# Pooled attention feeding a GELU feed-forward layer: w_in loaded in halves, and w_out with four rows in a run

## The chip, the cores and the metric

The kernel runs on one core of one Trainium2 chip. The metric is device microseconds from launch to end, lower is better; three runs of the kernel before gave 311.11, 311.66 and 311.69 us, median 311.66. Engine names are those of the profile: PE (matrix multiplications), PEld (the loading of their weights), DVE, ACT, POOL, and SP, which here only issues transfers.

## The reference, cut to what matters

Eight batches, eight heads, sequence 576, head size 64. Keys and values are pooled by means of 8 rows (576 to 72), attention is computed against the pooled rows, and the result, 4608 tokens by 512 channels, goes through two matrices with a GELU between them.

```python
k_p = k.reshape(B, H, Sp, pool, D).mean(axis=3)      # pool = 8, Sp = 72
v_p = v.reshape(B, H, Sp, pool, D).mean(axis=3)
scores = scale * np.matmul(q, k_p.transpose(0, 1, 3, 2))
attn = softmax(scores)                               # written out in the reference
x = np.matmul(attn, v_p)                             # then (B * S, H * D) = 4608 x 512
h = x @ w_in                                         # 512 x 2048
g = 0.5 * h * (1.0 + np.tanh(c * (h + 0.044715 * h * h * h)))
out = g @ w_out                                      # 2048 x 512, float32
```

## The kernel before, in words

**Stages.** The tokens are handled in nine groups of 512 (NG). Phase 1 of a group (`p1_mm`, L280 to L283) multiplies w_in by x: for each of 16 blocks of 128 hidden channels (fo) it accumulates four matmuls (ko, 128 input channels each). The weights of such a matmul are 128 columns of `w_in_b[:, ko, ...]`, the moving operand is 512 tokens of `xT`. `gelu` (L285) takes each block from PSUM to `gT`. Phase 2 (`p2_mm`, L290) multiplies `gT` by `w_out_b`: for each of four row blocks r it accumulates 16 matmuls, one for each fo, and `store` (L294) copies and writes the rows. The attention of batch nb = g + 1 is woven into group g: pooling additions on DVE (`k_steps`, `v_steps`, L145), transposes (`trans_k` L172, `trans_q` L189), scores (`qk` L211), exponentials (`expo` L218), weighted sums (`av` L231, for batch 0 L236), and the division (`norm`, `mult`).

**The start.** Batch 0 comes first. Sixteen dummy matmuls (`spin`, L312) open PE's program, and some more stand between the first transposes and scores. Then a loop over eight pairs (c, pr) runs `av`, `norm` and `mult` of batch 0; after pair 5 it issues 4, after pair 6 six and after pair 7 six of the sixteen "early" phase 1 matmuls of group 0 (L335 and L346: fo 0 to 3, first all with ko 0, then ko 1, and so on, 288 of the 512 tokens). Group 0 then does the other 224 tokens of fo 0 to 3, and fo 4 to 15 in full, with the pooling of batch 1 (DVE) and its transposes at set places in between. After pair 3 SP is given the loads of v for batch 1 (L345).

**The order of the work.** Each engine runs its instructions in the order in which the kernel writes them (`manual_schedule`, L46); waits are put in by the tile framework, which records which part of a tile an instruction reads or writes and makes a reader wait for the transfers that write a part it overlaps. Transfers that POOL issues share one software queue, and each uses the next of eight semaphores in turn, so that the ninth waits until the first has landed.

**Transfers that POOL issues at the start, in order (before):** q of batch 0 in two halves (L84), w_in columns 0 to 511 and 512 to 1023 (L103), then after five memsets k of batch 1 (L70, L71), q of batch 1, w_in columns 1024 to 1535 and 1536 to 2047, and w_out in four pieces of 512 rows (L139), then q of batch 2. SP issues half of k and all of v of batch 0, and v of batch 1. Both matrices are float32 in memory and bfloat16 in the tiles; the transfer converts them. One row of a w_in piece is 512 float32 values in memory, and so is a row of w_out: each run of a transfer reads 2 KB and writes 1 KB.

**Which piece which block needs (before).** w_in piece i serves fo 4i to 4i + 3. w_out piece i serves fo 4i to 4i + 3, and the first 32 matmuls of phase 2 in group 0 go through the pieces in that order (L419).

Of the kernel before, what the change touches and what calls it, by code (L numbers as in the profile page):

```python
# [18 lines left out]
def kernel(  # L19
# [9 lines left out]
    nc = tc.nc  # L29
# [29 lines left out]
    PS = psp.tile([128, 8, 512], F32, name="PS")  # L59
# [21 lines left out]
    def load_q(b, i0=0, i1=2):  # L81
        if b not in qs:
            qs[b] = qp.tile([128, 2, T * D], BF16, name="qb")
        nc.gpsimd.dma_start(  # L84
            out=qs[b][:, i0:i1],
            in_=q[b].rearrange("(i h) (p t) d -> (h p) i (t d)", i=2, t=T)[:, i0:i1])

    w_in_b = consts.tile([128, KO, DF], BF16, name="w_in_b")
    w_out_b = consts.tile([128, FO, DM], BF16, name="w_out_b")
    w_in_v = moe_w_in.rearrange("(ko p) f -> p ko f", p=128)  # L90
    w_out_v = moe_w_out.rearrange("(fo p) d -> p fo d", p=128)
    identb = consts.tile([128, 128], BF16, name="identb")


# [5 lines left out]
    make_identity(nc, identb)  # L100

    def load_w_in(i):
        nc.gpsimd.dma_start(out=w_in_b[:, :, i * 512:(i + 1) * 512], in_=w_in_v[:, :, i * 512:(i + 1) * 512])  # L103

    load_w_in(0)
    load_w_in(1)


    xT = consts.tile([128, KO, N], BF16, name="xT")
# [23 lines left out]

    load_k(1, [nc.gpsimd])
    load_q(1)
    load_w_in(2)
    load_w_in(3)
    for i in range(4):
        nc.gpsimd.dma_start(out=w_out_b[:, 4 * i:4 * i + 4, :], in_=w_out_v[:, 4 * i:4 * i + 4, :])  # L139


    qTs = {}
# [123 lines left out]
    def x_bank(g):  # L266
        return g % 2

    def h_bank(g, fo):
        x, y = x_bank(g), 1 - x_bank(g)  # L270
        if fo == 4:
            return 7
        return (x, 2, 3, y)[fo if fo < 4 else (fo - 1) % 4]
# [5 lines left out]

    def p1_mm(g, fo, ko, c0=0, c1=GROUP):  # L280
        r0 = g * GROUP
        nc.tensor.matmul(out=PS[:, h_bank(g, fo), c0:c1], lhsT=w_in_b[:, ko, fo * 128:(fo + 1) * 128],  # L282
                         rhs=xT[:, ko, r0 + c0:r0 + c1], start=(ko == 0), stop=(ko == KO - 1))  # L283

    def gelu(g, fo):  # L285
# [50 lines left out]
    for i, (c, pr) in enumerate(ORDER):  # L336
        bank = (4, 6, 0, 2, 4, 6, 4, 6)[i]
        av(0, c, pr, bank)
        norm(0, c, pr, bank)
        mult(0, c, pr, bank)  # L340
        if i == 3:

            vs[1] = kvp.tile([Sp, H, 512], F32, name="vt")
            nc.vector.memset(vs[1][:, 0, 0:1], 0.0)
            load_v(1, nc.sync)  # L345
        for fo, ko in early[:take[i]]:  # L346
            p1_mm(0, fo, ko, 0, CH)
        early = early[take[i]:]


    for g in range(NG):
# [34 lines left out]
        for fo, ko, c0 in first:  # L386
            p1_mm(g, fo, ko, c0)
        for fo in range(FO):
            if fo >= 4:
                for ko in range(KO):  # L390
                    p1_mm(g, fo, ko)
            gelu(g, fo)
            for s in side[fo]:
                s()
# [64 lines left out]
```

## Time and profile before

| what | value |
|---|---|
| time of the profiled execution | 311.66 us |
| its span, first to last instruction | 309.9 us |
| median of the three runs | 311.66 us |
| PE busy | 296.7 us, 96% |
| ACT busy, DVE busy | 220.9 us (71%), 157.1 us (51%) |
| phase 1 matmuls (L282), 128x512 | 379 ns each by the record, one every 216 ns |
| weight loads for them (L282, PEld) | 592 recorded, 98 ns each |
| transfers | 41.05 MB moved; 36.70 MB read, 9.44 MB written to memory |

The profiled execution's time is 1.8 us longer than its span. The matmuls overlap in PE's pipeline: a record of 379 ns includes the drain, and the starts of two matmuls of 512 tokens are 216 ns apart (seven of them make 1.51 us on the chain of waits). The weight loads run beside the matmuls. Landing times from the trace, in us from the start of the span (issue plus time to landing):

| transfer | issued | landed |
|---|---|---|
| w_in columns 0 to 511 | 3.0 | 16.6 |
| w_in columns 512 to 1023 | 3.8 | 18.6 |
| k of batch 1, main part | 8.1 | 21.7 |
| q of batch 1 | 9.2 | 25.8 |
| w_in columns 1024 to 1535 | 9.9 | 31.9 |
| w_in columns 1536 to 2047 | 10.7 | 36.6 |
| w_out, pieces 0, 1, 2, 3 | 11.8, 16.9, 18.9, 22.0 | 39.2, 41.6, 44.1, 46.7 |

### The profile page before, as it was taken

The page shows a single profiled execution, that of the slowest core. Times are in us where ns is not written, and L with a number is a line of the kernel's source. Part 1 is how long each engine was busy: PE and PEld are TensorE (multiplying, and loading weights), DVE is VectorE, ACT ScalarE, POOL GpSimd, SP SyncE. Part 2 cuts the span into 40 slices and gives each one's busy share as a digit, 9 for nine tenths or more (in the row PEclk, how much of TensorE's full clock was granted, in tenths as well). Part 3 has the DMA queues.
Part 4 walks back from the last instruction along what each step waited for, and adds up shares of the span by engine and source line. Part 5 has one row for each costly group of instructions (what it writes and reads, how often), then busy time and mean ns, then how long its engine had stood idle before and what let it go on. Part 6 is the DMA issues. An engine that isn't in the chain of part 4 may idle for free.

```text
span 309.9 us, 4249 instructions
## 1 busy us (share of the span) xinstructions
PE 296.7 (96%) x1516; PEld 149.5 (48%) x1545; DVE 157.1 (51%) x304; ACT 220.9 (71%) x414; POOL 30.8 (10%) x54
## 2 busy tenths in 40 slices
PE   7788899999999999999999999999999999999994
PEld 2455455444544455445544554455445544444441
DVE  3867536647568455855495358636772640020011
ACT  1597478877997799778987898689868987306500
POOL 8530000300301200030003000200000000000000
PEclk9999999999999999999999999999999999999999
DMA  7999995894895982588358826572101120121022
GB/s 225 232 279 249 178 200 116 266 225 87 258 224 113 237 186 62 112 225 175 85 110 232 185 68 100 166 182 68 41 0 33 49 56 0 36 68 34 2 68 69
DMA packets 32701, 41.05 MB, mean 132 GB/s; under 512 B 17608, under 2 KB 21704, under 8 KB 31784
## 3 DMA queue, kind: packets, MB, share of 16 engines
q0 software_dynamic: 10160, 24.26, 35.4%
q1 hardware_dynamic: 22200, 15.74, 21.8%
q10 hardware_dynamic: 320, 0.79, 0.8%
q8 instruction: 12, 0.20, 0.3%
q14 instruction: 9, 0.07, 0.1%
HBM read 36.70 MB, written 9.44 MB: 149 GB/s over the span
## 4 chain that ended last, share of the span: by engine, by line
PE 83%; DMA 12%; POOL 2%; issue 1%; ACT 0%; DVE 0%; POOLq 0%
PE PS L291 38%; PE PS L282 36%; DMA w_out_b<-in_moe_w_out_dram 8%; DMA kt<-in_k_dram 4%; PE PS L211 4%; PE PS L231 4%; PE PS L172 1%; POOL w_in_b L103 0%; POOL kT L128 0%; POOL qb L84 0%; POOL vp L131 0%; POOL vp L132 0%; DVE osb L296 0%; ACT e L218 0%; POOL kt L130 0%
## 5 line engine op out<-in xcount | busy, mean ns | idle before, releaser
L291 PE MATMUL PS<-w_out_b,gT 128*128 128x512 bf16 x560 | 133.8, 379 | 0.9
L282 PE MATMUL PS<-xT,w_in_b 128*128 128x512 bf16 (+2 forms) x580 | 128.3, 373 | 1.8 <-DMA w_in_b<-in_moe_w_in_dram 0.9
L288 ACT ACTIVATE gT<-PS 128x512 bf16<-128x512 f32 x144 | 81.3, 603 | 48.4 <-PE PS L282 48.2
L282 PEld LDWEIGHTS <-w_in_b 128*128 128x128 bf16 x592 | 57.2, 98 | 66.4 <-issue 2.0
L291 PEld LDWEIGHTS <-gT 128*128 128x128 bf16 x576 | 56.0, 97 | 57.1 <-issue 0.8
L296 DVE COPY osb<-PS 128x512 f32<-128x512 f32 x36 | 24.9, 692 | 94.9 <-PE PS L291 94.9
L257 DVE TENSOR_TENSOR xT<-PS,rc 64x288 bf16<-64x288 f32 (+1 forms) x120 | 54.6, 455 | 29.9 <-ACT rc L249 22.3
L218 ACT ACTIVATE e<-PS 72x576 bf16<-72x576 f32 x64 | 40.7, 644 | 8.4 <-PE PS L211 7.6
L145 DVE TENSOR_TENSOR vt<-vt 72x1024 f32<-72x1024 f32 (+1 forms) x32 | 30.5, 952 | 7.0 <-DMA vt<-in_v_dram 6.2
L249 ACT ACTIVATE rc<-ld 128x288 f32<-128x288 f32 x64 | 28.3, 443 | 2.1
L211 PE MATMUL PS<-qT,kT 128*72 128x288 bf16 x128 | 26.1, 286 | 0.4 <-ACT e L218 0.3
L244 ACT ACTIVATE ld<-PS 64x288 f32<-64x288 f32 x56 | 22.8, 408 | 1.4
L245 ACT ACTIVATE ld<-PS 64x288 f32<-64x288 f32 x56 | 22.5, 402 | 1.4
L263 ACT ACT_TABLE_LOAD x17 | 21.8, 1283 | 2.1 <-issue 1.8
L231 PE MATMUL PS<-e,vp 72*128 72x288 bf16 x112 | 23.1, 285 | 0.0
L211 PEld LDWEIGHTS <-kT 128*72 128x72 bf16 x128 | 14.4, 113 | 14.2 <-issue 1.4
L145 DVE TENSOR_TENSOR kt<-kt 128x1280 f32<-128x1280 f32 (+1 forms) x16 | 18.5, 1158 | 4.7 <-DMA kt<-in_k_dram 4.3
L358 POOL COPY gate<-qT 1x2 bf16<-1x2 bf16 x6 | 1.1, 176 | 155.8 <-DMA qT<-qb 155.8
L178 DVE COPY kT<-PS 64x504 bf16<-64x504 bf16 x15 | 10.1, 675 | 7.1 <-PE PS L172 7.0
L231 PEld LDWEIGHTS <-vp 72*128 72x128 bf16 x112 | 11.0, 98 | 3.3
L312 PE MATMUL PS<-idle 128*128 128x512 bf16 x28 | 9.6, 467 | 1.2 <-DVE idle L120 1.2
L145 DVE TENSOR_TENSOR vp<-vt 72x128 bf16<-72x128 f32 x28 | 6.9, 284 | 0.6
(45 smaller groups left out, 75.5 us busy)
## 6 DMA issues: line engine op xcount, KB each, us to landing
out_dram<-osb SPq DMA_DIRECT2D x142, 64.0 KB, 1.7
kt<-in_k_dram POOLq DMA_DIRECT2D x7, 1024.0 KB, 5.8
vt<-in_v_dram POOLq DMA_DIRECT2D x6, 1152.0 KB, 12.4
qb<-in_q_dram POOLq DMA_DIRECT2D x7, 576.0 KB, 15.1
w_in_b<-in_moe_w_in_dram POOLq DMA_DIRECT2D x4, 512.0 KB, 18.4
w_out_b<-in_moe_w_out_dram POOLq DMA_DIRECT2D x4, 512.0 KB, 25.0
vt<-in_v_dram SPq DMA_DIRECT2D x2, 512.0 KB, 11.1
vt<-in_v_dram SPq DMA_DIRECT2D x1, 1024.0 KB, 11.6
```

Of the source, the lines that this page charges most:

```text
L145: nc.vector.tensor_tensor(out=o, in0=a, in1=b, op=ALU.add)
L211: nc.tensor.matmul(out=PS[:Sp, bank + e, :CH].rearrange("j (t p) -> j t p", p=32), lhsT=kTs[b % 2][:, c, h, :], rhs=qTs[b][:, h // 4, :, h ...
L218: nc.scalar.activation(out=e, in_=PS[:Sp, bank:bank + 2, :CH], func=ACT.Exp, scale=1.0 / 64.0)
L231: nc.tensor.matmul(out=PS[:, bank + x, :CH], lhsT=flat(vps[b % 2][:, pr, x]), rhs=e[:, x, :], start=True, stop=True)
L244: nc.scalar.activation(out=ld[0:64], in_=PS[64:128, bank, :CH], func=ACT.Ln)
L245: nc.scalar.activation(out=ld[64:128], in_=PS[0:64, bank + 1, :CH], func=ACT.Ln)
L249: nc.scalar.activation(out=rc, in_=ld, func=ACT.Exp, scale=-1.0)
L257: nc.vector.tensor_tensor(out=xT[rows, pr, col:col + CH], in0=PS[rows, bank + x, :CH], in1=rc[rows], op=ALU.mult)
L282: nc.tensor.matmul(out=PS[:, h_bank(g, fo), c0:c1], lhsT=w_in_b[:, ko, fo * 128:(fo + 1) * 128], rhs=xT[:, ko, r0 + c0:r0 + c1], start=(ko ...
L288: nc.scalar.activation(out=gTs[g][:, fo, :], in_=PS[:, h_bank(g, fo), :], func=ACT.Gelu_apprx_tanh)
L291: nc.tensor.matmul(out=PS[:, o_bank(g, r), :], lhsT=gTs[g][:, fo, r * 128:(r + 1) * 128], rhs=w_out_b[:, fo, :], start=(fo == 0), stop=(fo ...
L296: nc.vector.tensor_copy(out=osb, in_=PS[:, o_bank(g, r), :])
```

## The change

w_in is loaded in two halves of 1024 columns in place of four quarters: a run reads 4 KB, the first half is issued where the first two quarters were, the second where the last two were. w_out is laid out so that partition p of a piece holds rows 4p to 4p + 3 of its 512 rows: a run reads 8 KB. To match, block fo = 4q + j of the hidden channels is now made of every fourth column, q * 512 + j + 4p for p from 0 to 127, so that the weights of a phase 1 matmul are read from `w_in_b` with a step of 4 elements instead of 1. Bytes, number and order of the matmuls stay. Line numbers of the changed kernel differ by at most one (w_in load L104, w_out load L138, the matmul of `p1_mm` keeps L282).

```diff
     w_in_v = moe_w_in.rearrange("(ko p) f -> p ko f", p=128)
-    w_out_v = moe_w_out.rearrange("(fo p) d -> p fo d", p=128)
+    w_out_v = moe_w_out.rearrange("(q p j) d -> p q (j d)", p=128, j=4)
...
     def load_w_in(i):
-        nc.gpsimd.dma_start(out=w_in_b[:, :, i * 512:(i + 1) * 512], in_=w_in_v[:, :, i * 512:(i + 1) * 512])
+        nc.gpsimd.dma_start(out=w_in_b[:, :, i * 1024:(i + 1) * 1024], in_=w_in_v[:, :, i * 1024:(i + 1) * 1024])

     load_w_in(0)
-    load_w_in(1)
...
     load_k(1, [nc.gpsimd])
     load_q(1)
-    load_w_in(2)
-    load_w_in(3)
+    load_w_in(1)
     for i in range(4):
-        nc.gpsimd.dma_start(out=w_out_b[:, 4 * i:4 * i + 4, :], in_=w_out_v[:, 4 * i:4 * i + 4, :])
+        nc.gpsimd.dma_start(out=w_out_b[:, 4 * i:4 * i + 4, :].rearrange("p j d -> p (j d)"), in_=w_out_v[:, i])
...
     def p1_mm(g, fo, ko, c0=0, c1=GROUP):
         r0 = g * GROUP
-        nc.tensor.matmul(out=PS[:, h_bank(g, fo), c0:c1], lhsT=w_in_b[:, ko, fo * 128:(fo + 1) * 128],
+        q, j = divmod(fo, 4)
+        nc.tensor.matmul(out=PS[:, h_bank(g, fo), c0:c1], lhsT=w_in_b[:, ko, q * 512 + j:(q + 1) * 512:4],
                          rhs=xT[:, ko, r0 + c0:r0 + c1], start=(ko == 0), stop=(ko == KO - 1))
```

## The prediction

> **What bounds the kernel now.** I read the page's engine shares and its chain of waits first, to see which engine sets the end and where it doesn't, then PE's timeline over the start, since that is the only stretch in which transfers stand on the chain.
>
> ```profile
> PE 296.7 (96%) x1516; PEld 149.5 (48%) x1545; DVE 157.1 (51%) x304; ACT 220.9 (71%) x414; POOL 30.8 (10%) x54
> ...
> PE 83%; DMA 12%; POOL 2%; issue 1%; ACT 0%; DVE 0%; POOLq 0%
> ```
>
> PE is busy for 96% of the span. The chain (second line) is PE but for 12% on transfers, all before 46.7 us. From there to 305.7 us PE runs without a wait that a load could shorten. So the change can act in two ways: through the start, where loads land, or through all 576 phase 1 matmuls, whose weights are now read with a step. PE's timeline from 20 to 40 us (start, length, engine, line, what, idle before):
>
> ```profile
> 20.67 0.29 PE L282 MATMUL PS<-xT,w_in_b 128*128 128x288 bf16 x1
> ...
> 22.24 0.90 PE L282 MATMUL PS<-xT,w_in_b 128*128 128x288 bf16 x6
> 22.98 0.41 PE L236 MATMUL PS<-e,ones 72*128 72x288 bf16 x2
> ...
> 32.01 1.04 PE L282 MATMUL PS<-xT,w_in_b 128*128 128x512 bf16 x4 [0.52 <-DMA w_in_b<-in_moe_w_in_dram]
> ...
> 36.57 3.63 PE L282 MATMUL PS<-xT,w_in_b 128*128 128x512 bf16 x16 [0.43 <-DMA w_in_b<-in_moe_w_in_dram]
> 40.03 1.46 PE L291 MATMUL PS<-w_out_b,gT 128*128 128x512 bf16 x6
> ```
>
> The first early phase 1 matmul runs at 20.67, the six after pair 6 at 22.24. PE waits for w_in only twice, 0.52 us at block 8 and 0.43 us at block 12: 0.95 us is all that faster loading of w_in can give back. The third w_in quarter landed at 31.9 and the last at 36.6.
>
> **A wait that the diff doesn't show.** I listed PE's instructions as the two kernels are built. They have the same 3092 rows but for the waits of w_in's weight loads. Before, these stand at blocks 0, 4, 8 and 12, one for each quarter. In the changed kernel there are two, and the second isn't at block 8:
>
> ```
> 185 L282 Ldweights w_in_b [waits DMASW2_49]
> ...
> 200 L235 Matmult PS<-e,vz 128x288
> 201 L282 Ldweights w_in_b [waits DMASW6_49]
> 202 L282 Matmult PS<-xT,w_in_b 128x288
> ```
>
> Counting POOL's transfers in turn over eight semaphores, number 2 is the first half of w_in and number 6 the second. Row 201 is the first early matmul after pair 6: block 0, ko 1, columns 0 to 508 by 4. It needs nothing of the second half. The framework takes the stepped slice to overlap it: in the tile, ko 1 starts at element 2048, between the second half's first element (1024) and its last, while ko 0 lies before it, and so only ko 1 is caught. Whatever the cause, the wait is in the program. PE runs in order, so all behind row 201 waits: pair 7, the early matmuls, group 0, and with pair 7 the DVE queue (its `mult`, then the pooling of k).
>
> **The parts, step by step.**
>
> 1. *When the second half lands.* The queue serves the same bytes in the same order, so I start from its pace. The transfers by queue, from 26 to 30 us and from 36 to 40 us (packets, MB, share of 16 engines):
>
> ```profile
> q1 hardware_dynamic: 346, 0.71, 63.7%
> q0 software_dynamic: 345, 0.34, 49.9%
> ```
>
> ```profile
> q0 software_dynamic: 823, 0.82, 123.9%
> ```
>
> Alone, a 2 KB run takes 4 us x 16 / 823 = 0.078 us of an engine; q's 256 runs of 4.6 KB, which land 2.8 us after w_out's last piece, take 0.175, so time goes by bytes and longer runs gain nothing. Beside v of batch 1 (q1) the queues take turns, 346 packets to 345, and a pair takes 4 x 16 / 345 = 0.185 us. With 4 KB runs a pair takes 0.185 + 0.078 = 0.263. The half has 512 runs, 32 for each engine, and begins when q of batch 1 is in, at 25.8. Alternating throughout: 25.8 + 32 x 0.263 = 34.2. Alone: 25.8 + 32 x 0.156 = 30.8. At the pace of before: 36.6. I take 34.2, since the row from 26 to 30 us shows the queues alternating.
>
> 2. *The stall.* Row 201 moves from 22.2 to 34.2: +12.0 us (8.6 to 14.4).
>
> 3. *What the stall hides.* The first half lands with the second quarter's time, 18.6, against a need at 20.67; with longer runs against v of batch 0 it takes more of the turns, so v may be a microsecond or two late (DVE waited 1.27 us for it at 16.5). All that ends before 34.2 and costs nothing; without the stall it would cost up to those 2 us. On POOL two issues of w_in go (0.78 us each), k and q of batch 1 are issued 0.8 us sooner, and the w_out issues lose waits of 4.43, 1.23 and 2.32 us, being now two places earlier in the turn of semaphores. The queue is already full (k landed 13.6 us after its issue), so I count 0. w_out's last piece, at 46.7, is needed after 50, and v of batch 1 after 45.
>
> 4. *What comes back.* The waits at blocks 8 and 12 go: -0.95. Late next is nothing that is loaded: group 0 then waits for DVE as before (0.96 us at the transposes of k).
>
> 5. *A cold PE.* The sixteen dummy matmuls at the start show PE slow after idleness; the windows view of that line (window, length, PE busy and count, weight loads, granted clock, DMA):
>
> ```profile
> 1.20:5.40 4.20, 4.20 (x10) 1.46 (x11) 1.00 0.78 274
> ```
>
> Ten starts in 4.2 us, 0.42 us each against 0.216 later, though the clock column reads 1.00. After the 2.0 us idle before 8.91 PE was fast at once (four dummies in 1.03 us). Ends: 0, as after 2.0 us idle; 10 x (0.42 - 0.216) = 2.0, as at the start. A stall of 12 us is nearer to the start. What the chain feels is less: ten matmuls up to pair 7 last 0.12 us more each, +1.2, then ACT and DVE work at their own pace while PE catches up within its 0.96 us wait. I take +1.2.
>
> [...]
>
> 6. *Stepped weight loads.* No row shows one. A contiguous load of 128 columns takes 98 ns, one of 72 columns (kT) 113 ns. If a stepped load goes at the slower pace by column, 113 x 128 / 72 = 201 ns, it is still below the 216 ns between matmuls and is hidden. Cover gone, it costs 576 x 98 ns = 56 us (a load end to end with its matmul). A gain is excluded, as the 98 ns are hidden already. I take 0.
>
> [...]
>
> 7. *w_out's 8 KB runs.* Same bytes, no gain by step 1, and covered to 50 us: 0.
>
> Sum against the profiled execution (311.66, span 309.9; also the median): 311.66 + 12.0 + 1.2 - 0.95 = **323.9 us**, slower by 3.9%. Ends: 311.66 + 8.6 - 0.95 = 319.3; 311.66 + 14.4 + 2.0 - 0.95 = 327.1.
>
> **The rivals.**
>
> - *The half lands with the last quarter's time, 36.6* (v's last rows, on eight partitions, slow both queues: 580 packets from 30 to 34 us against 691 in the four before): 311.66 + 14.4 + 1.2 - 0.95 = 326.3. Within the range.
> - *The wait binds only at block 8* (the change does what it says, row 201 costs nothing). PE reaches block 8 at 31.5: 311.66 + 34.2 - 31.5 - 0.95 = 313.4. Against it: the row stands in the program.
> - *Not slower: long runs speed the queue up.* The half must land by 22.2 for the gain of 0.95, and the time is 310.7; each microsecond later costs one, so it decides from 23.2. Against it: step 1's bytes by time; 2.1 MB more by 22 us, when q of batch 1 isn't in until 25.8.
> - *Weight loads uncovered:* 323.9 + 56 = 380, or a part of it from 216 ns on.
>
> **How the numbers follow.** Forecast 70%, landing at 36.6 15%, uncovered loads 7%, block 8 4%, long runs 3%, the rest above 328 1%. The range 319.3 to 327.5 holds the first two. A measurement of this kernel tells about 0.2% from no change. Faster 3% (long runs), slower 96%, same 1% (a part of the block 8 case, if the half lands two microseconds sooner).
>
> **What would show it.** One idle of PE of 10 to 14 us before a phase 1 matmul of 288 tokens, released by w_in's transfer, at 31 to 37 us; no PE wait for w_in at 512 tokens; some ten matmuls after it at twice the spacing; PEld of w_in at 201 ns or less; spacing 216 ns. It is wrong if PE passes 22 us without the wait, or if the 216 ns grow.

## The result, and the profile after

The changed kernel takes 319.25 us (median of four runs, 318.83 to 319.84) against 311.68 us (311.11 to 312.47): a ratio of 1.0243 with a 95% interval of 1.0213 to 1.0273, slower by 7.6 us. The forecast was 323.9, and the measured median lies just under its lower end of 319.3: the mechanism came, its size was overstated. The profiled execution took 319.6 us with a span of 317.8 us, 7.9 us more than the span before.

The page after: engine shares, the granted clock in 40 slices of 7.9 us, and the chain that ended last, which is now PE and one transfer of w_in.

```profile
PE 298.6 (94%) x1516; PEld 159.4 (50%) x1545; DVE 157.1 (49%) x304; ACT 220.8 (69%) x414; POOL 28.6 (9%) x52
...
PEclk9985799999999999999999999999999999999999
...
PE 87%; DMA 7%; POOL 2%; issue 1%; DVE 1%; ACT 0%; POOLq 0%
```

PE's timeline of the changed kernel over the start, with the idle time before each entry:

```profile
19.82 0.50 PE L235 MATMUL PS<-e,vz 72*128 72x288 bf16 x2 [1.53 <-DVE vz L144]
...
23.34 0.68 PE L235 MATMUL PS<-e,vz 72*128 72x288 bf16 x2
30.70 1.63 PE L282 MATMUL PS<-xT,w_in_b 128*128 128x288 bf16 x6 [6.68 <-DMA w_in_b<-in_moe_w_in_dram]
...
37.17 0.44 PE L171 MATMUL PS<-identb,kp 128*128 128x128 bf16 x5
...
43.00 5.34 PE L282 MATMUL PS<-xT,w_in_b 128*128 128x512 bf16 x23
48.18 1.46 PE L291 MATMUL PS<-w_out_b,gT 128*128 128x512 bf16 x6
```

The six early matmuls after pair 6 stand behind an idle of 6.68 us that w_in's transfer ends: they start at 30.70 where they started at 22.24. There is no wait for w_in at blocks 8 or 12 any more. Phase 2 begins at 48.18 instead of 40.03. From there on the two runs are alike but for one short wait of the run before.

Read along PE's program, the shift is 30.70 - 22.24 = 8.46 us at the stall, 37.17 - 27.73 = 9.44 at the transposes of k (0.98 for the slow clock), 48.18 - 40.03 = 8.15 at phase 2 (1.29 back, since the waits at blocks 8 and 12 are gone) and 7.9 at the end.

The last 0.3 us is a wait that the idle times of PE's timeline don't show and the chain of waits of the run before does (start, length, what):

```profile
21.97 24.72 DMA w_out_b<-in_moe_w_out_dram
46.69 0.04 issue
46.73 0.81 PE PS L291 x3
```

In the run before, the 25th matmul of phase 2 waits for w_out's last piece, which landed at 46.69. The matmul ahead of it started at 46.23, so at 0.216 us between starts it would have begun at 46.45: 0.28 us are lost. In the changed kernel this piece lands at 43.2, before phase 2 begins, and the same matmul starts at 54.59, 7.86 us later than before.

The granted clock by stretch (window, length, PE busy, PEld, DVE, ACT, POOL, then clock, DMA share, GB/s) shows something that the forecast did not have:

```profile
17.90:21.30 3.40, 1.87 (x16) 1.21 (x14) 3.13 (x7) 2.47 (x8) 0.93 (x2) 1.00 1.04 319
21.40:24.00 2.60, 2.60 (x12) 1.29 (x9) 1.38 (x4) 2.14 (x6) 0.20 (x1) 0.50 1.13 215
24.00:30.70 6.70, 0.02 (x1) 0.00 (x0) 0.46 (x1) 0.44 (x1) 0.00 (x0) 0.50 1.09 246
30.70:35.00 4.30, 4.29 (x19) 2.81 (x20) 1.23 (x2) 2.10 (x3) 0.00 (x0) 0.50 1.05 251
35.00:38.00 3.00, 2.95 (x26) 2.30 (x26) 2.29 (x4) 1.82 (x5) 0.00 (x0) 1.00 1.07 241
```

The clock falls to half at 21.4 us, before the stall and with PE busy 1.87 of the last 3.40 us, and comes back at 35.0, 4.3 us after the stall ends.

The weight loads with a step, at full clock (from 80 us on; minimum, median, maximum in ns), and the matmuls beside them:

```profile
L282 PEld LDWEIGHTS <-w_in_b x450: 112/113/118, 79.9 to 299.1; 128*128 128x128 bf16 x150
L282 PE MATMUL PS<-xT,w_in_b x443: 376/379/379, 79.7 to 299.3; 128*128 128x512 bf16 x148
```

A stepped load takes 113 ns instead of 98, and the matmuls still start every 216 ns (24 of them from 43.00 to 48.18): hidden, as counted.

### The profile page after: what moved, and what is told of

Same layout as the page of the kernel before. It is cut to its first block, busy times and chain, and to the rows that moved or that the text cites. A ratio compares the mean times of both kernels' runs of the same rounds, so it can differ in the third digit from the quotient of the medians.

```text
span 317.8 us, 4247 instructions
## 1 busy us (share of the span) xinstructions
PE 298.6 (94%) x1516; PEld 159.4 (50%) x1545; DVE 157.1 (49%) x304; ACT 220.8 (69%) x414; POOL 28.6 (9%) x52
## 3 DMA queue, kind: packets, MB, share of 16 engines
HBM read 36.70 MB, written 9.44 MB: 145 GB/s over the span
## 4 chain that ended last, share of the span: by engine, by line
PE 87%; DMA 7%; POOL 2%; issue 1%; DVE 1%; ACT 0%; POOLq 0%
PE PS L282 39%; PE PS L291 38%; DMA w_in_b<-in_moe_w_in_dram 7%; PE PS L210 4%; PE PS L230 4%; PE PS L171 1%; POOL qb L84 1%; DVE kT L177 0%; PE PS L188 0%; POOL kT L128 0%; PE PS L235 0%; POOL vp L131 0%; POOL vp L132 0%; POOL w_in_b L104 0%; DVE osb L296 0%
## 5 line engine op out<-in xcount | busy, mean ns | idle before, releaser
L282 PE MATMUL PS<-xT,w_in_b 128*128 128x512 bf16 (+2 forms) x580 | 130.1, 378 | 7.3 <-DMA w_in_b<-in_moe_w_in_dram 6.7
L282 PEld LDWEIGHTS <-w_in_b 128*128 128x128 bf16 x592 | 66.8, 114 | 64.6 <-DMA w_in_b<-in_moe_w_in_dram 7.2
L256 DVE TENSOR_TENSOR xT<-PS,rc 64x288 bf16<-64x288 f32 (+1 forms) x120 | 54.6, 455 | 38.2 <-ACT rc L248 30.7
L248 ACT ACTIVATE rc<-ld 128x288 f32<-128x288 f32 x64 | 28.3, 443 | 2.8 <-DVE xT L256 0.8
L230 PE MATMUL PS<-e,vp 72*128 72x288 bf16 x112 | 23.1, 285 | 0.0
L246 ACT ACTIVATE ld<-PS 128x288 f32<-128x288 f32 x8 | 3.2, 397 | 8.8 <-PE PS L235 8.8
## 6 DMA issues: line engine op xcount, KB each, us to landing
vt<-in_v_dram SPq DMA_DIRECT2D x1, 1024.0 KB, 16.2
```

The lines of the kernel that those rows point to most:

```text
L230: nc.tensor.matmul(out=PS[:, bank + x, :CH], lhsT=flat(vps[b % 2][:, pr, x]), rhs=e[:, x, :], start=True, stop=True)
L248: nc.scalar.activation(out=rc, in_=ld, func=ACT.Exp, scale=-1.0)
L256: nc.vector.tensor_tensor(out=xT[rows, pr, col:col + CH], in0=PS[rows, bank + x, :CH], in1=rc[rows], op=ALU.mult)
```

## The theories

**A.** The loss is PE's wait at the first early matmul with ko 1, a wait for the second half that the data does not ask for. **B.** The stepped weight loads cost it. **C.** The halves cost it as such, since block 8 must wait for more bytes. Later came the question why the half landed at 30.7 us and not at 34.2: **F**, the long runs of the first half bring the whole queue forward; **G**, only the second half's own runs do.

## The experiments

### Two tiles: the change without the wait

```diff
-    w_in_b = consts.tile([128, KO, DF], BF16, name="w_in_b")
+    w_in_h = [consts.tile([128, KO, DF // 2], BF16, name=f"w_in_h{i}") for i in range(2)]
...
-        nc.gpsimd.dma_start(out=w_in_b[:, :, i * 1024:(i + 1) * 1024], in_=w_in_v[:, :, i * 1024:(i + 1) * 1024])
+        nc.gpsimd.dma_start(out=w_in_h[i], in_=w_in_v[:, :, i * 1024:(i + 1) * 1024])
...
-                         lhsT=w_in_b[:, ko, q * 512 + j:(q + 1) * 512:4],
+                         lhsT=w_in_h[q // 2][:, ko, q % 2 * 512 + j:(q % 2 + 1) * 512:4],
```

> The whole change, but with w_in's two halves in two tiles, so that a stepped slice can only overlap its own half. Theory A (the loss is PE's wait at the first early matmul with ko 1, which needs nothing of the second half): the wait of 6.7 us goes, the second half lands near 30.7 us as in the changed kernel and is needed only after 31.5, so block 8 waits 0 us. What is left of the loss is v of batch 0 about 1 us late and PE's clock at half from 21.4 us for some 4 us (1 to 2 us), less the 0.95 us that blocks 8 and 12 waited before: 311.7 to 312.8 us, 312.2 the likeliest, against 319.25 of the change and 311.68 before. Rival B (the loss is the stepped weight loads, 113 against 98 ns): it stays, 319. Rival C (the halves as such, block 8 waiting for the second half): 313 or more, with a PE wait of 1 us or more at block 8.

Measured: 312.72 us against 311.72 (1.0041, 1.0021 to 1.0060). The half landed at 30.6 as in the change, no wait for it is left, and 6.5 of the 7.6 us are gone: theory A. B and C fall, because the steps and the halves are all still there. What waits PE has (engine, what, released by, us, times, longest):

```profile
PE PS L188 <- DMA qb<-in_q_dram: 2.5, 2, 1.9
PE PS L235 <- DVE vz L144: 2.3, 1, 2.3
```

The 1 us that remains stands ahead of group 0: v of batch 0 is late (an idle of 2.3 us for it, 0.81 before), and the clock falls after it.

### Halves alone, adjoining columns, short runs of w_out

```diff
-    w_out_v = moe_w_out.rearrange("(q p j) d -> p q (j d)", p=128, j=4)
+    w_out_v = moe_w_out.rearrange("(fo p) d -> p fo d", p=128)
...
-    lhsT=w_in_b[:, ko, q * 512 + j:(q + 1) * 512:4]
+    lhsT=w_in_b[:, ko, fo * 128:(fo + 1) * 128]
```

> The halves of w_in alone: weights by adjoining columns as before, w_out by 2 KB runs as before. Theory A: the waits are exact again (block 0 and block 8), and so no stall: the same as the two tiles, 311.7 to 312.8 us. If the stepped loads of weights cost anything that is not hidden, this one is faster than the two tiles by that much; theory A says by less than 0.3 us, rival B by 7 us. If w_out's longer runs gave anything, this one is slower than the two tiles.

Measured: 313.83 us (1.0065, 1.0049 to 1.0081), no stall, so A again. It is 1.1 us slower than the two tiles, which was not expected. Neither profile has a wait for w_out; in this one the clock was at half for 6.8 us (21.4 to 28.3), in the two-tile one for 3.4 (22.4 to 25.8). The last experiment takes this up.

### Quarters with stepped columns

The change, with w_in loaded in four quarters as before:

```diff
-        nc.gpsimd.dma_start(out=w_in_b[:, :, i * 1024:(i + 1) * 1024], in_=w_in_v[:, :, i * 1024:(i + 1) * 1024])
+        nc.gpsimd.dma_start(out=w_in_b[:, :, i * 512:(i + 1) * 512], in_=w_in_v[:, :, i * 512:(i + 1) * 512])
...
     load_w_in(0)
+    load_w_in(1)
...
-    load_w_in(1)
+    load_w_in(2)
+    load_w_in(3)
```

> The stepped columns and w_out's four rows in a run, with w_in loaded in four quarters as before. Theory A: the first early matmul with ko 1 now waits for the second, third and fourth quarter, the last of which landed at 36.6 us before; the stall is 36.6 - 22.2 = 14.4, plus 1 for the half clock, less 1.2 for waits that vanish: 325.9 us, 7 us slower than the change, with one PE idle of 12 to 14 us before a matmul of 288 tokens. If the long runs are what brought the landing forward in the changed kernel (q of batch 1 at 23.1 instead of 25.8), it is near 36.6 here; if not, nearer to 31, and the time near 319. Rival C (the halves cost): 312, no stall.

Measured: 325.24 us (1.0433, 1.0414 to 1.0452). The built program has at the same matmul a wait for the second, third and fourth quarter, and PE stands for the last of them, which lands at 36.2:

```profile
36.24 1.63 PE L284 MATMUL PS<-xT,w_in_b 128*128 128x288 bf16 x6 [12.72 <-DMA w_in_b<-in_moe_w_in_dram]
```

So it is the step that makes the false wait, and the landing that sets its length. With short runs the landing is at 36.2, with long ones at 30.7: the longer loads, by landing earlier, hid 6 us of the loss that the step makes.

### Dummies during the stall

```diff
         mult(0, c, pr, bank)
...
+        if i == 6:
+            spin(20)
         for fo, ko in early[:take[i]]:
```

> The change with 20 more dummy matmuls on PE right before the stalled matmul, so that PE is busy during the stall instead of idle; they add work that the output does not need, and should end by about 30.4 us. Theory A (half clock after the stall costs about 1 us of the 7.6): the clock is full when the second half lands at 30.7, the 35 matmuls behind the stall go at full pace, and the time is 318.2 us. Rival D (the half clock hides behind DVE's pooling of k, which waits in the same place): 319.2, no change. If the dummies last beyond the landing it is slower by the excess.

Measured: 318.54 us (1.0223, 1.0203 to 1.0243), 0.7 us less than the change. The transposes of k start 35.90 - 30.38 = 5.52 us after the stall, as before the change (27.73 - 22.24 = 5.49); without the dummies it was 6.47. So the slow clock behind the stall costs about 1 us in the profiles, and by them D falls. The medians alone would not decide it: 0.7 us apart, with runs from 318.28 to 319.34 here and from 318.83 to 319.84 in the change.

### Short runs first: why the half landed at 30.7

```diff
-    load_w_in(0)
+    load_w_in(0, 512)
+    load_w_in(512, 1024)
...
-    load_w_in(1)
+    load_w_in(1024, 2048)
```

> The change (one tile, stepped weights, the stall in place) with the first half of w_in loaded in two quarters of 2 KB runs and the second half in one piece. It tells why the second half landed at 30.7 us and not at the 34.2 of the forecast. Theory F (the longer runs of the first half bring the whole queue forward, since they lose less beside v of batch 0; q of batch 1 landed at 23.1 in the change, at 25.5 and 25.8 with quarters): q of batch 1 lands at 25.5 here, the second half 7.4 us later at 32.9, and the time is 319.25 + 2.2 = 321.5 us. Theory G (only the second half's own runs matter, through its turns beside v of batch 1): it still lands near 30.7 to 31.2 and the time is 319.3 to 319.8.

Measured: 321.86 us (1.0325, 1.0289 to 1.0361). q of batch 1 landed at 25.3 and the half at 32.9, 7.6 us after it (7.5 in the change): theory F, on both numbers. The wait in PE's timeline:

```profile
33.04 1.60 PE L283 MATMUL PS<-xT,w_in_b 128*128 128x288 bf16 x6 [9.36 <-DMA w_in_b<-in_moe_w_in_dram]
```

Where the long runs win is seen while w_in's first part (q0) shares the transfer engines with v of batch 0 (q1). The transfers by queue from 10 to 14 us (packets, MB written, share of 16 engines), before the change and then after it:

```profile
q1 hardware_dynamic: 312, 0.58, 60.3%
q0 software_dynamic: 360, 0.37, 55.8%
```

```profile
q0 software_dynamic: 268, 0.54, 70.6%
q1 hardware_dynamic: 273, 0.53, 39.1%
```

In the same 4 us w_in moved 0.54 MB in place of 0.37, and v 0.53 in place of 0.58: the queues still took turns (268 packets to 273, and 360 to 312 before), each packet of w_in carried twice as much (2.0 KB for 1.0), and the two together moved 1.07 MB in place of 0.95 in less busy time (109.7% for 116.1%). Why the short runs are so much slower in this company is not settled.

The packets also show that w_in's third quarter didn't begin at one moment. A packet of w_in in quarters writes 1 KB and one of q 2.3 KB. In the trace before, from 22 to 24 and from 24 to 26 us:

```profile
DMA packets 235, 0.42 MB, mean 209 GB/s; under 512 B 12, under 2 KB 98, under 8 KB 234
DMA packets 388, 0.48 MB, mean 239 GB/s; under 512 B 5, under 2 KB 305, under 8 KB 388
```

So 98 - 12 = 86 packets of w_in's third quarter moved by 24 us and 300 more by 26, while q of batch 1, issued ahead of it, was not all in before 25.8.

### Dummies at the late v, two tiles

```diff
     for i, (c, pr) in enumerate(ORDER):
+        if i == 2:
+            spin(4)
```

> The two tiles with 4 dummy matmuls on PE ahead of pair 2, where PE waits 2.3 us for v of batch 0 there; they are extra work that the output does not need and fit inside that wait. Theory H (in the two-tile run the 1.0 us over the kernel before is the clock, which fell to half from 22.4 to 25.8 us after that wait): the clock stays full and the time is 311.2 to 311.7 us, against 312.7. Rival (the loss is v's lateness itself, the clock hides behind DVE and ACT): 312.7, no change, or 0.2 slower if the dummies push pair 2 back.

Measured: 311.94 us (1.0019, 0.9998 to 1.0039): no longer to be told from the kernel before. The clock stayed full through the profile (a mean of 1.000), and phase 2 began at 39.71 instead of 41.38. The medians, 0.8 us apart, are not enough for theory H, since the intervals of the two ratios overlap. The mean granted clock of the single runs supports it: 0.997 or more in ten of the twelve runs here, 0.991 or less in all six of the two tiles without dummies. The runs spread from 311.20 to 314.20, and the two slowest are the two with the lower clock (0.991 and 0.987).

### v of batch 0 in the turn ahead of w_in, two tiles

```diff
-    load_v(0, nc.sync, 4, 8)
     load_q(0, 0, 1)
     load_q(0, 1, 2)
+    load_v(0, nc.gpsimd, 4, 8)
```

The load keeps its two parts of 64 and 8 partitions.

> The two tiles, with the second half of v of batch 0 issued by POOL between q of batch 0 and w_in instead of by SP, so that w_in's long runs no longer take turns from it. If v's lateness and the clock that falls after it are all that is left of the change's loss, v lands by about 14 us, the wait for it at pair 2 shrinks from 2.3 us to nothing, the clock stays full, and the 0.95 us that blocks 8 and 12 waited before is gained: 310.4 to 311.0 us, faster than the kernel before (311.7). If q of batch 0 or k of batch 1 is pushed back by it, or block 8 waits, 311.7 or more.

Measured: 313.38 us (ratio without the slowest run 1.0055, 1.0030 to 1.0081), twelve runs from 312.10 to 317.49; without the slowest the median is 313.00. A miss. v did arrive in time and its wait went, but the clock fell all the same, in the profile from 20.4 to 23.9 us, and block 8 now waited 0.60 us for the half, which landed at 32.8. The wide spread of the runs stays unexplained; the clock alone does not order them (313.76 us at a mean of 0.996, 312.66 at 0.990).

### v of batch 1 later, in the change

```diff
-        if i == 3:
+        if i == 6:
```

> The change with v of batch 1 issued after pair 6 instead of pair 3, some 2.5 to 3 us later, so that the second half of w_in has the transfer engines to itself for longer. The forecast's pace (0.156 us of an engine for a 4 KB run alone, 0.263 for a pair with one of v) gives about 28.9 us for its landing in place of 30.7, and 319.25 - 1.8 = 317.5 us, the stall shrinking one for one. Rival (the turns beside v do not set the landing): 319.2. If v of batch 1 is then late for DVE at block 10 the gain is less.

Measured: 318.35 us (1.0214, 1.0185 to 1.0244). The half landed at 29.1 (28.9 expected) in place of 30.7, 5.3 us after q of batch 1 where 32 runs at 0.156 us make 5.0: the pace alone is right, and the rival falls. The transfers from 24 to 29 us hold no packet of q1 at all:

```profile
q0 software_dynamic: 470, 1.07, 111.4%
```

So nothing of v ran beside the half here, and in the change its turns cost some 7.5 - 5.3 = 2.2 us. The time fell by 0.9 us in the medians and 1.7 in the profiled spans (316.1 against 317.8); half of the expected 1.8 is not seen in the medians, whose intervals overlap, so I leave open how much of it is real.

### Two more, to see whether anything beats the kernel before

> The two tiles with the 4 dummy matmuls, and v of batch 1 issued after pair 1 instead of pair 3. In the run without this PE waited 0.54 us in group 0's second phase for v of batch 1, and the second half of w_in, landed at 30.4, was needed only at 32.3. With v of batch 1 some 1.5 us sooner that wait goes and the half lands by about 31.3, still in time: 311.4 us, at or just under the kernel before (311.5). If the half is pushed past 32.3, or the clock falls, 311.9 or more.

Edit: `if i == 3` to `if i == 1` in the two-tile kernel with dummies. Measured: 311.42 us (1.0003, 0.9983 to 1.0022): no difference from the kernel before. The 0.54 us wait is gone; the profiled run, at 312.69 us, had a mean clock of 0.993, ten of the other eleven 0.997 or more.

> Halves of w_in with adjoining columns and w_out by 2 KB runs (the second experiment), with the same 4 dummy matmuls ahead of pair 2 as in the two-tile run that had them. They are extra work that the output does not need. If the 1.1 us between the two-tile run and the plain halves (312.72 and 313.83) was the clock, which stayed at half for two windows in the one profile and one in the other, both are alike once the clock is held: 311.9 us within 0.4. If w_out's longer runs or the stepped weights were the reason, the difference of 1.1 us stays: 313.

Edit: the four dummies in the kernel with halves alone. Measured: 311.25 us (0.9998, 0.9976 to 1.0020). With the clock held (a mean of 0.999 in its profile) the plain halves are no slower than the two tiles with the step, so the 1.1 us between the first two experiments was the clock. The single runs say the same: a mean clock of 0.997 or more in eleven of the twelve here, 0.986 to 0.989 in all six without dummies, and the twelfth run here, at 0.986, took 314.00 us.

The median is 0.7 us below that of the two tiles with the same dummies, and below the 311.9 within 0.4 that was expected. The intervals of the two ratios overlap, but the profiles have a cause: w_out's long runs hold up v of batch 1. PE in phase 2 and DVE at the first addition of v, two tiles with dummies:

```profile
43.93 0.50 PE L230 MATMUL PS<-e,vp 72*128 72x288 bf16 x2 [0.54 <-DVE vp L144]
41.53 1.94 DVE L144 TENSOR_TENSOR vt<-vt 72x1024 f32<-72x1024 f32 x2 [6.31 <-DMA vt<-in_v_dram]
```

and DVE in the plain halves with dummies:

```profile
37.46 1.95 DVE L144 TENSOR_TENSOR vt<-vt 72x1024 f32<-72x1024 f32 x2 [2.19 <-DMA vt<-in_v_dram]
```

v was issued at 22.2 us in both, took 16.6 us beside w_out's long runs and 12.1 beside the short ones (16.2 and 12.4 in the same two kernels without dummies), and the wait of 0.54 us stands only in the first. In the change itself the stall covers it: phase 2 begins at 48.18. No version tried beats the kernel before.

## Why the prediction was right about the way and wrong about the size

- **The wait at row 201** (the step "a wait that the diff doesn't show"): right. It is one idle of PE before a matmul of 288 tokens, ended by w_in's transfer; two tiles take it away, and 6.5 of 7.6 us with it. The quarters with a step show that the slice with a step makes it, not the size of the half.
- **When the second half lands** (step 1): this is the step that failed. It put the landing at 34.2; it was 30.65. The first 2.7 us of the error are the start: "begins when q of batch 1 is in, at 25.8" was taken over from the trace before, and the longer runs let q land at 23.1 (25.3 when the first half went back to short runs). The reason given for it, "time goes by bytes and longer runs gain nothing", came from stretches in which w_out and q had the transfer engines to themselves, and did not hold beside v (0.54 MB in place of 0.37 in the same 4 us). Nor did w_in's third quarter wait until q, ahead of it, was all in, as its 86 packets by 24 us show. The other 0.9 us is the time beside v of batch 1, 7.5 us for the half against 8.4 with v in every turn. In the change v, itself issued 1 us later, has no packet under way before 26 us. But with short runs first v was issued at 21.2 us as in the kernel before, and the half took 7.6 us all the same, so what makes up these 0.9 us stays open.
- **The stall** (step 2): one for one with the landing, 8.46 us against 12.0, and 12.72 us of idle in the run with quarters.
- **What the stall hides** (step 3): right for v. v of batch 0 landed 1.0 us later and cost nothing in the change, though it does cost once the stall is gone. Wrong for w_out: "w_out's last piece, at 46.7, is needed after 50" does not hold in the trace before, where PE would have used it at 46.45.
- **What comes back** (step 4): 1.29 us for 0.95. A record of a matmul is 379 ns long where starts in a running stream are 216 ns apart, so after an idle the next start is late by that idle and by some 0.16 us more, twice. Another 0.29 us came back in phase 2, where PE no longer waits for w_out's last piece; so "late next is nothing that is loaded" was wrong too. The wait for DVE at the transposes of k, 0.96 us before, is gone as well, because PE arrives there late at its slow clock.
- **A cold PE** (step 5): 0.98 us for 1.2, right in size, and the dummies confirm it in the profiles (6.47 against 5.52). The ten matmuls up to pair 7 took 33.09 - 30.70 = 2.39 us in place of 23.47 - 22.24 = 1.23, which is the 1.2 of the forecast. The reason was half right: PE was slow after the stall, but the clock had fallen before it, at 21.36 us, after 3.40 us in which PE was busy for 1.87 (and in the run with v in its turn for 2.63).
- **Stepped weight loads** (step 6): right. 113 ns instead of 98, below the bound of 201 and hidden below 216.
- **w_out's long runs** (step 7): 0 in the change, but not because they are "covered to 50 us": w_out had 0.28 us to give back before, and its long runs put v of batch 1 off by some 4 us. The stall covers that here; with stall and slow clock gone it costs a wait of 0.54 us.

With the measured parts, the sum of the forecast would have been 311.66 + 8.46 + 0.98 - 1.29 - 0.29 = 319.5, against 319.6 for the profiled execution. That the lower end of the range, 319.3, came so near is luck: it let the half run alone from 25.8 and so had it in at 30.8, close to the 30.65 measured, from a start 2.7 us too late and a stretch 2.5 us too short (5.0 against 7.5). It also left out the clock's 0.98 us and 0.6 of what came back, which partly cancel. At the other end the sum gives 327.1, and the range was put at 327.5 without a term for the difference.

## What to carry to other kernels

When a slice gets a step, list the waits of the program as it is built: a dependency tracker may take a stepped slice for more than it reads, and the cost is the whole time to that transfer's landing; two tiles, or adjoining columns, make the wait exact. A landing time from the old trace is no anchor for a transfer whose neighbours in the queue change too: recompute the queue from its first changed transfer on, and take the pace from a stretch with the same company. Longer runs on one queue put off what another carried here (v of batch 1 took 16.6 us to land in place of 12.1), so look at who needs that. When you call a load covered, find the instruction that uses it first: here the chain of waits named w_out's last piece, while PE's idle times did not. And look at the granted clock by windows before calling a wait hidden: in the two tiles, after a wait of 2.33 us in a stretch with PE busy for 2.09 of 3.30 us, it was at half for 3.4 us.

## What the runs showed of the hardware

- **The clock fell with PE busy for over half of the 3.3 to 3.4 us before.** The run with two tiles (windows, same columns as above):

```profile
19.00:22.30 3.30, 2.09 (x15) 1.51 (x16) 2.75 (x8) 1.62 (x5) 0.58 (x1) 1.00 1.08 231
22.40:25.70 3.30, 3.30 (x15) 2.01 (x15) 1.37 (x3) 1.80 (x5) 0.03 (x1) 0.50 1.11 211
25.80:30.00 4.20, 3.55 (x29) 2.80 (x28) 2.94 (x4) 3.85 (x7) 0.00 (x0) 1.00 1.09 254
```

  PE was busy 2.09 of 3.30 us, mostly with matmuls of 72 rows of the array, and the clock was then at half for 3.4 us. In the change it was at half for 13.65 us, from 21.36 to 35.01, after 1.87 of 3.40 us. Runs of one kernel differ in it: of 46 runs of the kernel before, the 21 with a mean clock of 0.997 or more have a median of 311.04 us, the 11 with 0.989 or less 312.35. Why the clock falls in one run and not in another is not settled, nor what share of work holds it: the kernel before kept it with 2.32 of 3.40 us, the run with v in its turn lost it with 2.63, so the busy share alone does not decide.
- **Longer runs landed sooner where queues mixed.** w_in's last byte landed at 36.2 to 36.6 us in quarters, at 32.9 with the second half in one piece and at 30.3 to 30.9 with both (in the runs that issue both v as the change does), at the same bytes, while alone a run of 2 KB (0.078 us of an engine) and one of 4.6 KB (0.175) moved at the same rate. The other queue paid: v of batch 1 took 16.6 us to land beside w_out's 8 KB runs and 12.1 beside 2 KB runs.
- **A step of four 2-byte elements in the stationary operand cost 15 ns a load**, 113 against 98.
